# Moving the last four shifted pieces of the first token mix into the plan that orders the attention

## The chip, the cores and the metric

The kernel runs on one core of one Trainium2 chip. Its time is the device time of one execution in microseconds (us); the engines named below are those of that core: TensorE (PE; its weight loads are PEld), VectorE (DVE), ScalarE (ACT), GpSimd (POOL) and SyncE (SP), which issues the transfers (DMA) in queue order.

## What is computed

Three stages in a row. First an attention over 2 batches x 8 heads, 768 tokens, head size 64, with a mask made of hashed sign bits; then a channel mix with a shift by one token; then a low-rank mix over the tokens and a wide two-layer network.

```python
mask = q_bucket[:, :, :, None] == k_bucket[:, :, None, :]
scores = np.where(mask, scale * q @ k.T, -1e9)          # softmax, then @ v -> x [2, 768, 512]
x_prev = x shifted down by one token
xk = mu_k * x + (1.0 - mu_k) * x_prev
xr = mu_r * x + (1.0 - mu_r) * x_prev
k = np.maximum(xk @ w_k, 0.0)                           # 512 -> 1024
v = k * k @ w_v                                         # 1024 -> 512
x = sigmoid(xr @ w_r) * v
u = x + (x.T @ U @ V).T
out = u + np.maximum(u @ w_ch1, 0.0) @ w_ch2            # 512 -> 2048 -> 512
```

The inputs q, k, v and the weights come as 64-bit words or 32-bit floats. A product of 32-bit accuracy is made of three products of halves: high x high, high x low, low x high.

## The kernel before, in words

**Attention.** 16 heads x 6 tiles of 128 query rows. For each head q and k are loaded (`nq`, `nk`), split into halves (`hl_q`, `hl_k`), transposed by TensorE and copied to `yq`, `yk`; `xq`, `xk` and `zt` hold the rows with the bits. These are the prepared q and k, which only the scores (L521, L522) read. The results of two heads form one block of 128 features of x, `xn`, which TensorE transposes (L616) in two steps of three products each; ScalarE evicts each step to `xT` (L389). All these transposes go through one PSUM bank, tag `t`, which is free again only after the eviction.

**The plan.** Everything up to the end of the attention is added to a list of operations (`Plan.add`) with engines and costs, dependences, buffers taken and freed, and a due time: the place in the attention plus an offset from the table `DUE` by kind. `Plan.order` walks through time and gives each free engine the ready operation with the smallest due time. The program is then written in that order, and every engine runs its own part strictly in it. Where the plan sees a gap of TensorE it adds idle products (L332) in number to the gap's length.

**The first mix, its shifted pieces.** For batch 0 there are 16 pieces `(s, g, c)`: `s` is r or k (xr or xk), `g` a half of the tokens (384), `c` one of four blocks of 128 features. A piece takes four instructions: a scaling of the shifted x (`shift_scaled`, L716 on ScalarE or L718 on VectorE) into an `xs_a` buffer of the tag `sq` (3 buffers, shared with the activations below), the sum on VectorE (`shift_sum`, L722), the high half on ScalarE (`shift_high`, L737) and the low half (`shift_low`, L180, on POOL or VectorE). The plan holds the first twelve: r of both halves, and k of the first half. The last four, k of the second half of the tokens, are called k1c0 to k1c3 here. The pool `xh2` holds their halves, and it is opened after the attention's pools are closed.

**The first mix, its products.** Units u = 0 to 15: `m = u // 2` is a block of 128 of the 1024 hidden features, `g = u % 2` the half of the tokens. A k half, k(u), is 12 products of 384 columns (3 for each `c`); ScalarE makes a relu and a square, POOL the exact square, VectorE the low half (L796); a v half, v(u), is nine products of 512 columns, of which the third is the first to read the low half. The order is k(0), k(2), v(0), k(1), v(2), k(3), v(1), and so on, so that k(1) is the first to read k1c0 to k1c3. They are made by a loop that stands between k(0) and the rest:

```python
mix.acc()
k_half(mix, 0, True)
while mix.todo or mix.begun:
    shifts(mix, nc.gpsimd if len(mix.todo) % 2 else None)
halves(mix, u1, range(1, U1 - 2), ...)
```

**Weights.** They arrive as 64-bit words in 512 KB loads (`raw`, 3 buffers) and are converted in jobs: ScalarE two scalings (L224, L225), VectorE two steps on the bits (L229, L233), POOL a sum (`cx`, L180), ScalarE the high half (L273), VectorE or POOL the low half. The jobs run as a chain: with each k half of the mix one step of four jobs and one load is taken ("tick"). The plan converts jobs 0 to 7, which serve w_r and the units 0 to 3, and starts the next ones; the first tick, in k(0), has the halves of job 8, the sum of job 9, the bits of job 10, the scalings of job 11 and the load of job 12, which goes into the buffer that the sum of job 9 frees.

Of the kernel before, what the change touches and what calls it, by code (L numbers as in the profile page):

```python
# [22 lines left out]
PE_TILES = (1, 4)  # L23
# [6 lines left out]
JOB_GATE = (0, 0, 1, 1, 2, 3, 4, 5)  # L30
JOBS = 8
VG = 4
FILL, FIRST_FILL = 0.85, 34
SLOTS = {"s": 3, "t": 1, "o": 1, "n": 4, "hl_q": 1, "hl_k": 1, "y_q": 2, "y_k": 2, "x_q": 2, "x_k": 2, "zt": 2,
         "p": 3, "p12": 4, "pT": 6, "xn": 2, "raw": 3, "cx": 4, "xh": 4, "sq": 3, "v": 2, "nm": 4, "nv": 6}
# [94 lines left out]
def lsh_attention_moe_kernel(  # L130
# [19 lines left out]
    nc = tc.nc  # L150
# [150 lines left out]
    def load_head(i, s, eng=None):  # L301
        b, h = heads[i]
        src = {"k": k, "q": q, "v": v}[s]
        if s == "v":
            t = NV[i % len(NV)][:, :, 0:D]
        else:
            t = hd[i]["n" + s] = ap.tile([128, NT, D], F32, tag=f"n{s}", name=f"n{s}")
        (eng or nc.sync).dma_start(out=t, in_=src[b, h].rearrange("(p t) d -> p t d", t=NT))
# [67 lines left out]
    big = ap.tile([VG, 128], F32, name="big", bufs=1)  # L376
# [21 lines left out]
    def prep_H(i, s, e):  # L398
        t = hd[i]["hl" + s] = ap.tile([128, NT, 2, D], F32R, name=f"hl_{s}", bufs=1)
        copy(e, t[:, :, PART[s]], hd[i]["n" + s])  # L400
# [19 lines left out]
    def prep_E(i, s, g, e):  # L420
        if g == 0:
            hd[i]["y" + s] = ap.tile([128, S], F32R, tag=f"y{s}", name=f"y{s}")
        copy(e, hd[i]["y" + s][:, g * G:(g + 1) * G], hd[i].pop(("t" + s, g)))

    def first_E(s, e):
        hd[0]["y" + s] = ap.tile([128, S], F32R, tag=f"y{s}", name=f"y{s}")
        copy(e, hd[0]["y" + s].rearrange("p (g c) -> p g c", g=NG), hd[0]["both" + s][:, :, 0:G])

    def first_x(s, e):
        t = hd[0]["x" + s] = ap.tile([MC, S], F32R, tag=f"x{s}", name=f"x{s}")  # L430
        copy(e, t[LOW].rearrange("p (g c) -> p g c", g=NG), hd[0].pop("both" + s)[HI[s], :, 0:G])
# [10 lines left out]
    def prep_x(i, s):  # L442
        t = hd[i]["x" + s] = ap.tile([MC, S], F32R, tag=f"x{s}", name=f"x{s}")
        nc.sync.dma_start(out=f(t)[LOW], in_=f(hd[i]["y" + s])[HI[s]])
# [10 lines left out]
    def prep_bits(i):  # L455
        zt = hd[i]["zt"] = ap.tile([ZE, G], F32R, tag="zt", name="zt")
# [10 lines left out]

    vg = [{} for _ in range(NH // VG)]

    def v_max(i):  # L470
        g, j = divmod(i, VG)
        if j == 0:
            vg[g]["max"] = ap.tile([128, VG], F32, tag="vmax", name="vmax")
        nc.vector.tensor_reduce(
            out=vg[g]["max"][:, j:j + 1], in_=NV[i % len(NV)][:, :, 0:D], axis=AX.XY, op=ALU.max, apply_absolute_value=True
        )

    def v_flip(g):
# [12 lines left out]
    def v_spread(g):
        vg[g]["u"] = psum_t()
        nc.tensor.matmul(vg[g]["u"][:, 0:VG], big, vg[g].pop("pow"), start=True, stop=True)

    def v_scale(g):
        sc = vg[g]["scale"] = ap.tile([128, VG], F32, tag="vsc", name="vsc", bufs=3)
        nc.vector.tensor_copy(sc, vg[g].pop("u")[:, 0:VG])

    def v_scale_of(i):
        g, j = divmod(i, VG)  # L500
        return vg[g]["scale"][:, j:j + 1]
# [11 lines left out]

    def scores(n):
# [52 lines left out]

    def flip_out(n, e):
        pT = tl[n]["pF"] = ap.tile([128, NT, 128], F32, tag="pT", name="pF", bufs=SLOTS["pT"])
        copy(e, pT.rearrange("p (j i) c -> p j (i c)", j=NG), tl[n].pop("f")[:, :, 0:G])  # L570


    def weighted(n):
# [4 lines left out]
        if t in PE_TILES:  # L578
# [340 lines left out]
    for i in range(NH):  # L919
# [38 lines left out]
        g, j = divmod(i, VG)  # L958
# [3 lines left out]
        if j == VG - 1:  # L962
            at0 = g * VG * NT - 4
            t_s, u_s = Slot("t"), Slot("t")
            fl = add({"pe": 0.2}, lambda e, g=g: v_flip(g), v_mx[-VG:], at0, take=[t_s], lag=0.25)
# [3 lines left out]
            for ii in range(g * VG, i + 1):  # L969
                v_s2, nv_s2 = v_slots[ii]  # L970
                v0 = v0_of[ii] = add({"act": 0.62}, lambda e, i=ii: prep_v(i, 0), [v_sc, v_ld[ii]], ii * NT - 0.5, "v1")
                v1 = add({"act": 0.53}, lambda e, i=ii: prep_v(i, 1), [v0], ii * NT, "v1", [v_s2])
                v2_of[ii] = add({"pool": 0.98}, lambda e, i=ii: prep_v(i, 2), [v1], ii * NT, "v2", free=[nv_s2])
    for i in range(NH):
# [3 lines left out]
        for t in range(NT):  # L978
# [9 lines left out]
            if t in PE_TILES:  # L988
# [3 lines left out]
                got = add({"act": 0.83, "dve": 0.86}, lambda e, n=n: flip_out(n, e), [fl], n, "f1", [pT_s], [f_s])  # L992
# [5 lines left out]
            on_pe = t in PE_TILES  # L998
            avs.append(add({"pe": 0.9 if on_pe else 0.62}, lambda e, n=n: weighted(n), [got, v0_of[i] if on_pe else v2], n, "av",
# [37 lines left out]
    for j, (s, g, c) in enumerate(todo := mx0.todo[0:3 * KD]):  # L1037
        a_s = Slot("sq")
        if c == 0:
            x_s = [Slot("xh") for _ in range(KD)]  # L1040
# [3 lines left out]
        hi = add({"act": 0.53}, lambda e, p=p: hold.append(mx0.shift_high(*p)), [sm, hi and low_of[todo[j - 1]]], at, kind, [x_s[c]])  # L1044
# [19 lines left out]
    mx0.todo = mx0.todo[3 * KD:]  # L1064
# [8 lines left out]
    late["xh2"] = pool(mix_s, "xh2", side="right", bufs=4)  # L1073
# [38 lines left out]
    while mix.todo or mix.begun:  # L1112
        shifts(mix, nc.gpsimd if len(mix.todo) % 2 else None)
# [111 lines left out]
```

## Time and profile before

| what | value |
|---|---|
| three runs of the kernel | 728.95, 730.35, 734.12 us; median 730.35 |
| the profiled execution | 728.76 us, of which the span from first to last instruction is 727.0 |
| busy share of the span | PE 97%, PEld 84%, DVE 61%, ACT 53%, POOL 48% |
| mean granted clock of TensorE | 0.995 of 2.4 GHz |
| chain that ended last | PE 75%, DVE 8%, POOL 5%, DMA 4%, issue 4%, ACT 3% |

Times in rows are us from the span's start. In a timeline row stand start, length, engine, line, operation, what is written from what, shape and count, and in brackets the idle time just before it with what ended it. A waits row names who waited for whom, then the total, the number of waits and the longest. A windows row has the stretch, its length, the busy time (and count) of PE, PEld, DVE, ACT and POOL, then the granted clock (1.00 is 2.4 GHz, 0.50 is 1.2 GHz), the DMA share and GB/s. Starts are those of the profiler; the length of a TensorE product is modelled, so its pace is read from start to start.

### The profile page before, as it was taken

What the parts mean: (1) busy time and instruction counts of PE and PEld (TensorE: products, weight loads), DVE (VectorE), ACT (ScalarE), POOL (GpSimd) and SP (SyncE); (2) the same over time, 40 slices, a digit from 0 to 9 for tenths busy, and PEclk for the clock granted to TensorE, in tenths of its full rate; (3) what the DMA queues carried; (4) which work ended last, traced back from release to release, by engine and by line L of the source; (5) the groups of instructions that cost most, each with busy time, mean ns of one, the idle gap of its engine ahead of it and who ended that gap; (6) DMA issues with size and microseconds to landing.
All of it is one profiled execution on the core that took longest, in us unless ns stands there. A gap on an engine that the chain in (4) does not pass through costs nothing.

```text
span 727.0 us, 12722 instructions
## 1 busy us (share of the span) xinstructions
PE 707.1 (97%) x4907; PEld 612.1 (84%) x4907; DVE 440.6 (61%) x791; ACT 385.2 (53%) x651; POOL 351.1 (48%) x309
## 2 busy tenths in 40 slices
PE   9899999999999998999999999999999999999997
PEld 8798999999999886889788888778888888888886
DVE  7987888677776656898879978655532111321112
ACT  5887888688878666666478566434421001110100
POOL 5998888787969855566357544613300000000000
PEclk9999999999999999899999999999999999999999
DMA  7899899996987961322013332323201000010001
GB/s 189 194 177 198 190 198 205 167 175 148 174 182 144 208 114 58 116 75 92 2 59 115 116 114 63 125 77 109 65 0 59 1 0 1 1 58 1 0 1 58
DMA packets 140715, 73.23 MB, mean 101 GB/s; under 512 B 116832, under 2 KB 134064, under 8 KB 140656
## 3 DMA queue, kind: packets, MB, share of 16 engines
q1 hardware_dynamic: 140512, 72.24, 43.2%
q8 instruction: 38, 0.62, 0.3%
q10 hardware_dynamic: 144, 0.20, 0.1%
q14 instruction: 21, 0.17, 0.1%
HBM read 37.10 MB, written 3.15 MB: 55 GB/s over the span
## 4 chain that ended last, share of the span: by engine, by line
PE 75%; DVE 8%; POOL 5%; DMA 4%; issue 4%; ACT 3%; SPq 0%; POOLq 0%; ACTq 0%; DVEq 0%
PE ps L807 9%; PE pt L807 9%; PE ps L809 9%; PE pt L809 9%; PE pt L808 9%; PE ps L808 9%; PE pt L581 3%; DMA pT<-p 3%; PE pt L587 3%; PE ps L521 3%; POOL p L180 2%; PE ps L522 2%; PE pt L453 2%; DVE w L180 2%; PE pt L415 1%
## 5 line engine op out<-in xcount | busy, mean ns | idle before, releaser
L882 DVE SCALAR_TENSOR_TENSOR hl<-pt,hl 128x512 fp32r<-128x512 f32 x48 | 33.2, 691 | 170.9 <-ACT hl L881 170.9
L881 ACT ACTIVATE hl<-pt 128x512 fp32r<-128x512 f32 x48 | 28.7, 598 | 185.1 <-PE pt L809 185.1
L809 PE MATMUL ps<-w,hl 128*128 128x512 f32 x288 | 114.3, 397 | 3.3 <-DVE hl L796 3.1
L807 PE MATMUL ps<-w,hl 128*128 128x512 f32 x288 | 115.7, 402 | 0.1
L808 PE MATMUL ps<-w,hl 128*128 128x512 f32 x288 | 113.9, 395 | 0.0
L180 POOL TENSOR_TENSOR cx<-cx,raw 128x512 int32<-128x512 int32 (+2 forms) x55 | 80.4, 1461 | 65.2 <-DVE cx L233 59.2
L180 POOL TENSOR_TENSOR p<-p,p 128x768 f16<-128x768 f32 x64 | 108.0, 1693 | 7.8 <-ACT p L389 5.9
L526 DVE TENSOR_REDUCE nm<-ps 128x1 f32<-128x768 f32 x96 | 90.5, 952 | 17.3 <-PE ps L522 15.9
L540 ACT ACTIVATE p<-ps,nm 128x768 f32<-128x768 f32 x96 | 92.9, 988 | 11.7 <-DVE nm L534 10.3
L807 PE MATMUL pt<-ut,w 128*128 128x512 f32 x192 | 75.6, 394 | 0.0
L809 PE MATMUL pt<-ut,w 128*128 128x512 f32 x192 | 75.0, 391 | 0.0
L808 PE MATMUL pt<-ut,w 128*128 128x512 f32 x192 | 75.0, 391 | 0.0
L521 PE MATMUL ps<-xk,xq 76*128 76x384 f32 x192 | 70.6, 368 | 1.9 <-ACT p L540 1.2
L809 PEld LDWEIGHTS ps<-w,hl 128*128 128x128 f32 x288 | 54.5, 189 | 19.2 <-DVE hl L796 7.1
L807 PEld LDWEIGHTS ps<-w,hl 128*128 128x128 f32 x288 | 54.5, 189 | 14.1 <-issue 1.7
L180 DVE TENSOR_TENSOR w<-cx,w 128x512 fp32r<-128x512 f32 (+2 forms) x52 | 61.2, 1177 | 8.2 <-ACT w L273 7.7
L522 PE MATMUL ps<-yk,yq 128*128 128x384 f32 x192 | 65.1, 339 | 0.0
L808 PEld LDWEIGHTS ps<-w,hl 128*128 128x128 f32 x288 | 54.6, 190 | 10.3
L229 DVE SCALAR_TENSOR_TENSOR raw<-raw 128x512 uint32<-128x512 uint32 (+2 forms) x55 | 54.2, 985 | 0.0
L180 POOL TENSOR_TENSOR sq<-sq 128x384 f32<-128x384 f32 x32 | 32.0, 1000 | 38.2 <-ACT hl L791 37.2
L391 POOL CAST p<-p 128x768 f16<-128x768 f32 x49 | 41.3, 843 | 17.1 <-ACT p L540 15.8
L587 PE MATMUL pt<-v,pT 128*128 128x65 f16 (+1 forms) x1152 | 45.7, 194 | 2.5 <-DMA pT<-p 2.5
(181 smaller groups left out, 1511.5 us busy)
## 6 DMA issues: line engine op xcount, KB each, us to landing
raw<-in_moe_w_ch_dram SPq DMA_DIRECT2D x32, 512.0 KB
raw<-in_moe_w_k_dram SPq DMA_DIRECT2D x8, 512.0 KB
raw<-in_moe_w_v_dram SPq DMA_DIRECT2D x8, 512.0 KB
nk<-in_k_dram SPq DMA_DIRECT2D x16, 192.0 KB
nv<-in_v_dram SPq DMA_DIRECT2D x16, 192.0 KB
nq<-in_q_dram SPq DMA_DIRECT2D x15, 192.0 KB
xk<-yk SPq DMA_DIRECT2D x15, 192.0 KB
xq<-yq SPq DMA_DIRECT2D x15, 192.0 KB
```

Of the source, the lines that this page charges most:

```text
L180: eng.tensor_tensor(out=out, in0=a, in1=b, op=op)
L229: nc.vector.scalar_tensor_tensor(out=raw[:, :, 0], in0=raw[:, :, 1], scalar=0x80000000, in1=raw[:, :, 0], op0=ALU.bitwise_and, op1=ALU.bit ...
L391: (nc.vector if e == "dve" else nc.gpsimd).tensor_copy(dst, src)
L521: nc.tensor.matmul(s_ps[:, j, 0:G], d["xq"][:, qc], d["xk"][:, c], start=True, stop=False)
L522: nc.tensor.matmul(s_ps[:, j, 0:G], d["yq"][:, qc], d["yk"][:, c], start=False, stop=True)
L526: nc.vector.tensor_reduce(out=nm[:, 0:1], in_=tl[n]["s"][:, :, 0:G], axis=AX.XY, op=ALU.max, negate=True)
L540: nc.scalar.activation(p, tl[n].pop("s")[:, :, 0:G], AF.Exp, bias=nm[:, 2:3], scale=nm[:, 1:2])
L587: nc.tensor.matmul(o[:, 0:d], pT[:, part, kt, :], V[:, kt, a, 0:d], start=(kt == 0 and (part, a) == (0, 0)), stop=(kt == NT - 1 and part = ...
L807: nc.tensor.matmul(o, sh, mh, start=first, stop=False)
L808: nc.tensor.matmul(o, sh, ml, start=False, stop=False)
L809: nc.tensor.matmul(o, sl, mh, start=False, stop=last)
L882: nc.vector.scalar_tensor_tensor(out=hl[:, 1], in0=self.o, scalar=0.0, in1=f(hl)[:, 0], op0=ALU.max, op1=ALU.subtract)
```

## The change

All sixteen pieces of batch 0 are now in the plan. The last four have the kind `m3`, whose offset 900 puts them behind everything else that is ready. Their halves still go to the pool `xh2`, which is now opened, on the other side of the memory, in the moment in which the last scores are written into the program: the prepared q and k have a pool of their own (`prep`) that is closed there, and the high halves of the last four pieces carry a dependence on all scores and flips (`last_s`). The loop behind k(0) is gone.

```diff
-       "r4": -59.5, "r5": -145.5}
+       "r4": -59.5, "fw": 4.7, "f2": 0, "m3": 900, "r5": -145.5}
...
+    prep_s = ExitStack()
     ap = pool(att, "att", side="right", bufs=2)
+    pp = pool(prep_s, "prep", side="right", bufs=2)
...
     def scores(n):
...
+        scored.append(n)
+        if len(scored) == NH * NT:
+            prep_s.close()
+            late["xh2"] = pool(mix_s, "xh2", bufs=4)
...
-    for j, (s, g, c) in enumerate(todo := mx0.todo[0:3 * KD]):
+    for j, (s, g, c) in enumerate(todo := mx0.todo):
         a_s = Slot("sq")
         if c == 0:
-            x_s = [Slot("xh") for _ in range(KD)]
+            far = (s, g) == ("k", 1)
+            x_s = [Slot("xh2" if far else "xh") for _ in range(KD)]
         at, kind, p = 2 * c, f"m{j // KD}", (s, g, c)
         begun = [add({"act": 0.6 if g else 0.85}, lambda e, p=p: mx0.shift_scaled(*p, e == "act"), begun, at, kind, [a_s])]
         sm = add({"dve": 1.1}, lambda e, p=p: mx0.shift_sum(*p), begun, at, kind)
-        hi = add({"act": 0.53}, lambda e, p=p: hold.append(mx0.shift_high(*p)), [sm, hi and low_of[todo[j - 1]]], at, kind, [x_s[c]])
+        hi = add({"act": 0.53}, lambda e, p=p: hold.append(mx0.shift_high(*p)), [sm, hi and low_of[todo[j - 1]], *(last_s if far else [])],
+                 at, kind, [x_s[c]])
         low_of[p] = add({"pool": 1.05}, lambda e, p=p: mx0.shift_low(*p, hold.pop(), nc.gpsimd), [hi], at, kind, free=[a_s])
...
-    mx0.todo = mx0.todo[3 * KD:]
+    mx0.todo = []
...
-    late["xh2"] = pool(mix_s, "xh2", side="right", bufs=4)
...
     mix.acc()
     k_half(mix, 0, True)
-    while mix.todo or mix.begun:
-        shifts(mix, nc.gpsimd if len(mix.todo) % 2 else None)
     halves(mix, u1, range(1, U1 - 2), ...)
```

The rest of the diff renames: `PE_TILES = (1, 4)` becomes `MODES` with the same two tiles on TensorE, `VG = 4` becomes `GROUPS = (4, 4, 4, 4)`, the tiles `n`, `hl`, `y`, `x` and `zt` of q and k are taken from `prep`, and the scale of v has four buffers instead of three. A third way for a tile ("F") is written and not used.

On ScalarE, at the attention's end, the rows before run from the high half of the third k piece (`xh`) over four evictions (`xT`) to the high half of weight job 8 (`w`) and the relu of k(0) (`sq`):

```order
L737 ACTIVATE xh_4827<-xs_a_4646 128x384
L389 ACTIVATE xT_154<-pt_4831 128x384
L737 ACTIVATE xh_4854<-xs_a_4797 128x384
L389 ACTIVATE xT_154<-pt_4857 128x384
L389 ACTIVATE xT_154<-pt_4879 128x384
L389 ACTIVATE xT_154<-pt_4894 128x384
L273 ACTIVATE w_4937<-cx_4588 128x512
L790 ACTIVATE sq_4942<-pt_4924 128x384
```

The same place on ScalarE after the change, from the high half of the fourth k piece to the high half of job 8 (the scaling of k1c0 stands just ahead of the first of the four evictions, which is the one before these rows):

```order
L764 ACTIVATE xh_4864<-xs_a_4804 128x384
L743 ACTIVATE xs_a_4871<-xT_154,omu_k_326 128x384
L391 ACTIVATE xT_157<-pt_4867 128x384
L764 ACTIVATE xh_4879<-xs_a_4837 128x384
L743 ACTIVATE xs_a_4905<-xT_154,omu_k_326 128x384
L391 ACTIVATE xT_157<-pt_4901 128x384
L764 ACTIVATE xh_4931<-xs_a_4871 128x384
L743 ACTIVATE xs_a_4933<-xT_155,omu_k_326 128x384
L391 ACTIVATE xT_157<-pt_4927 128x384
L764 ACTIVATE xh_4938<-xs_a_4905 128x384
L764 ACTIVATE xh_4941<-xs_a_4933 128x384
L275 ACTIVATE w_4979<-cx_4591 128x512
```

A scaling and a high half now stand ahead of each of the last three evictions, and two high halves ahead of the weights.

On POOL the rows before run from the low half of the fourth k piece over the sum of job 9 (`cx`) and the square for k(0) (`sq`) to two of the last four pieces, the sum of job 10 and the square for k(2):

```order
L180 TENSOR_TENSOR xh_4854<-xs_a_4797,xh_4854 128x384
L180 TENSOR_TENSOR cx_4657<-cx_4657,raw_4477 128x512
L180 TENSOR_TENSOR sq_4942<-sq_4942 128x384
L180 TENSOR_TENSOR xh_4960<-xs_a_4954,xh_4960 128x384
L180 TENSOR_TENSOR xh_4972<-xs_a_4963,xh_4972 128x384
L180 TENSOR_TENSOR cx_4674<-cx_4674,raw_4479 128x512
L180 TENSOR_TENSOR sq_4996<-sq_4996 128x384
```

The same place on POOL after the change:

```order
L180 TENSOR_TENSOR xh_4864<-xs_a_4804,xh_4864 128x384
L180 TENSOR_TENSOR xh_4879<-xs_a_4837,xh_4879 128x384
L180 TENSOR_TENSOR xh_4931<-xs_a_4871,xh_4931 128x384
L180 TENSOR_TENSOR xh_4938<-xs_a_4905,xh_4938 128x384
L180 TENSOR_TENSOR xh_4941<-xs_a_4933,xh_4941 128x384
L180 TENSOR_TENSOR cx_4664<-cx_4664,raw_4480 128x512
L180 TENSOR_TENSOR sq_4984<-sq_4984 128x384
L180 TENSOR_TENSOR cx_4681<-cx_4681,raw_4482 128x512
L180 TENSOR_TENSOR sq_5014<-sq_5014 128x384
```

All four low halves, two of which were VectorE's, stand ahead of the sum of job 9 and the square for k(0). On VectorE the four sums stand ahead of the weights of job 8 now, one of them ahead of the last head's normalisation; two scalings and two low halves are gone from it. TensorE has 7 idle products more ahead of each of the last two pairs of transposes (28 rows with their weight loads), and nothing else moved on it. SP's order is the same.

## Rows read from the trace of the kernel before

**Rows 1.** The page: busy time, share of the span and instructions of each engine.

```profile
PE 707.1 (97%) x4907; PEld 612.1 (84%) x4907; DVE 440.6 (61%) x791; ACT 385.2 (53%) x651; POOL 351.1 (48%) x309
```

**Rows 2.** Waits of TensorE over the whole span: total, times, longest.

```profile
PE ps L809 <- DVE hl L796: 3.1, 5, 0.9
```

**Rows 3.** Timeline of PE, 274 to 301 us, end of attention and first mix.

```profile
274.81 0.69 PE L332 MATMUL pt<-steady 128*128 128x120 f16 x10
...
275.56 0.55 PE L616 MATMUL pt<-ident,xn 128*128 128x128 f32 x3
...
275.86 0.42 PE L807 MATMUL pt<-xh,w 128*128 128x384 f32 x1
...
280.13 0.39 PE L807 MATMUL ps<-w,hl 128*128 128x512 f32 x1
...
280.97 0.50 PE L809 MATMUL ps<-w,hl 128*128 128x512 f32 x1 [0.22 <-DVE hl L796]
...
282.68 0.34 PE L807 MATMUL pt<-xh,w 128*128 128x384 f32 x1
...
288.42 0.63 PE L807 MATMUL ps<-w,hl 128*128 128x512 f32 x1
...
293.42 0.52 PE L807 MATMUL pt<-xh,w 128*128 128x384 f32 x1
...
296.01 0.40 PE L807 MATMUL ps<-w,hl 128*128 128x512 f32 x1
...
300.15 0.39 PE L807 MATMUL ps<-w,hl 128*128 128x512 f32 x1
```

**Rows 4.** Windows of 1 us: the granted clock in the first mix.

```profile
287.00:288.00 1.00, 0.42 (x2) 0.38 (x2) 1.00 (x2) 0.97 (x4) 0.15 (x1) 0.83 0.00 0
...
288.00:289.00 1.00, 1.00 (x4) 0.75 (x3) 1.00 (x3) 1.00 (x2) 0.87 (x1) 0.50 0.79 147
...
294.00:295.00 1.00, 1.00 (x6) 1.00 (x6) 1.00 (x1) 0.00 (x0) 1.00 (x1) 0.75 0.27 93
```

**Rows 5.** Timeline of ACT: last eviction, a scaling, a high half.

```profile
276.14 0.49 ACT L389 ACTIVATE xT<-pt 128x384 f32<-128x384 f32 x1 [0.64 <-PE pt L616]
...
280.37 0.60 ACT L716 ACTIVATE xs_a<-xT,omu_k 128x384 f32<-128x384 f32 x1
...
282.64 0.52 ACT L737 ACTIVATE xh<-xs_a 128x384 fp32r<-128x384 f32 x1
```

**Rows 6.** Timeline of POOL, 273 to 290 us: lows, weight sums, squares.

```profile
273.13 1.00 POOL L180 TENSOR_TENSOR xh<-xs_a,xh 128x384 fp32r<-128x384 f32 x1 [2.98 <-ACT xh L737]
...
274.08 1.29 POOL L180 TENSOR_TENSOR cx<-cx,raw 128x512 int32<-128x512 int32 x1
...
279.50 0.83 POOL L180 TENSOR_TENSOR sq<-sq 128x384 f32<-128x384 f32 x1 [4.13 <-ACT hl L791]
...
282.26 1.22 POOL L180 TENSOR_TENSOR xh<-xs_a,xh 128x384 fp32r<-128x384 f32 x1 [1.93 <-ACT xh L737]
...
285.53 1.62 POOL L180 TENSOR_TENSOR cx<-cx,raw 128x512 int32<-128x512 int32 x1
...
288.13 1.33 POOL L180 TENSOR_TENSOR sq<-sq 128x384 f32<-128x384 f32 x1 [0.98 <-POOL cx L180]
```

**Rows 7.** Timeline of DVE, 280 to 294 us: low halves, piece sums, weight low.

```profile
280.36 0.56 DVE L796 TENSOR_TENSOR hl<-sq,hl 128x384 fp32r<-128x384 f32 x1 [1.54 <-POOL sq L180]
...
281.99 1.91 DVE L722 SCALAR_TENSOR_TENSOR xs_a<-xT,mu_k,xs_a 128x384 f32<-128x384 f32 x2
...
290.13 1.78 DVE L180 TENSOR_TENSOR w<-cx,w 128x512 fp32r<-128x512 f32 x1
...
293.40 0.55 DVE L796 TENSOR_TENSOR hl<-sq,hl 128x384 fp32r<-128x384 f32 x1
```

**Rows 8.** Timeline of SP: the load of weight job 12.

```profile
275.40 0.38 SPq L212 DMA_DIRECT2D raw<-in_moe_w_k_dram  x1
```

**Rows 9.** Windows: a stretch of the attention with a long TensorE hole.

```profile
60.00:62.00 2.00, 0.56 (x16) 0.40 (x14) 0.00 (x0) 0.81 (x1) 1.73 (x3) 1.00 1.05 112
```

More of the change, by code (lines that the diff above doesn't have):

```diff
@@ L21 @@
 P_SHIFT = 12.0 * math.log(2.0)
-PE_TILES = (1, 4)
+MODES = ("DWDDWD", "DWDDWD")
 DUE = {"ld": -28.3, "h": 7, "lo": 111.2, "tr": -11.5, "es": -25.5, "xs": 92.5, "z": -68.8, "bits": 0,
@@ L375, in lsh_attention_moe_kernel @@
         V2.append(t)
-    big = ap.tile([VG, 128], F32, name="big", bufs=1)
+    big = ap.tile([max(GROUPS), 128], F32, name="big", bufs=1)
     nc.gpsimd.memset(big, 2.0 ** 13)
@@ L455, in prep_bits @@
     def prep_bits(i):
-        zt = hd[i]["zt"] = ap.tile([ZE, G], F32R, tag="zt", name="zt")
+        zt = hd[i]["zt"] = pp.tile([ZE, G], F32R, tag="zt", name="zt")
         nc.vector.tensor_scalar(
@@ L466, in prep_mask @@
             )
-    vg = [{} for _ in range(NH // VG)]
+    vg = [{} for _ in GROUPS]
+    vg_of = [(g, j) for g, n in enumerate(GROUPS) for j in range(n)]
+    VG = max(GROUPS)
     def v_max(i):
-        g, j = divmod(i, VG)
+        g, j = vg_of[i]
         if j == 0:
@@ L566, in flip, with mode @@
                 nc.tensor.transpose(f_ps[:, j, c], p[:, j, c], ident)
+    def mode(n):
+        return MODES[n // (NT * H)][n % NT]
     def flip_out(n, e):
@@ L570, in flip_out, with flipped, flip_part1, flip_part2 @@
         copy(e, pT.rearrange("p (j i) c -> p j (i c)", j=NG), tl[n].pop("f")[:, :, 0:G])
+    def flipped(n, part):
+        return tl[n]["pT"][:, part].rearrange("p (j i) c -> p j (i c)", j=NG), tl[n]["f"][:, :, 0:G]
+    def flip_part1(n):
+        pT_tile(n)
+        p1, src = flipped(n, 0)
+        nc.scalar.activation(p1, src, AF.Copy)
+    def flip_part2(n):
+        p1, src = flipped(n, 0)
+        minus("dve", flipped(n, 1)[0], src, p1)
+        tl[n].pop("f")
     def weighted(n):
@@ L968, in lsh_attention_moe_kernel @@
             v_sc = add({"dve": 0.15}, lambda e, g=g: v_scale(g), [sp], at0, free=[u_s])
-            for ii in range(g * VG, i + 1):
+            for ii in range(i0, i + 1):
                 v_s2, nv_s2 = v_slots[ii]
@@ L987, in lsh_attention_moe_kernel @@
             ex = add({"act": 1.02}, lambda e, n=n: exps(n), [bi], n, "ex", [p_s], [s_s, nm_s])
-            if t in PE_TILES:
+            kind = mode(n)
+            if kind in "FW":
                 f_s = Slot("s")
@@ L991, in lsh_attention_moe_kernel @@
                 last_s.append(fl)
-                got = add({"act": 0.83, "dve": 0.86}, lambda e, n=n: flip_out(n, e), [fl], n, "f1", [pT_s], [f_s])
+            if kind == "F":
+                p1 = add({"act": 0.83}, lambda e, n=n: flip_part1(n), [fl], n, "f1", [pT_s])
+                got = add({"dve": 0.97}, lambda e, n=n: flip_part2(n), [p1], n, "f2", free=[f_s])
+            elif kind == "W":
+                got = p1 = add({"act": 0.83, "dve": 0.86}, lambda e, n=n: flip_out(n, e), [fl], n, "fw", [pT_s], [f_s])
             else:
@@ L997, in lsh_attention_moe_kernel @@
                 got = add({"sp": 2.2}, lambda e, n=n: transp(n), [p2], n, "T", [pT_s], [c_s], issue=1.45)
-            on_pe = t in PE_TILES
-            avs.append(add({"pe": 0.9 if on_pe else 0.62}, lambda e, n=n: weighted(n), [got, v0_of[i] if on_pe else v2], n, "av",
+            avs.append(add({"pe": 0.9 if kind == "W" else 0.62}, lambda e, n=n: weighted(n), [got, v0_of[i] if kind == "W" else v2], n, "av",
                            [] if avs else [o_s], [pT_s, v_s, v_slots[i][1]], lag=0.25))
```

47 lines of the change are left out of this document (25 added, 22 removed).

## The prediction

> **What bounds the kernel now.** I read the page's busy line first: TensorE is busy for 97% of the span [rows 1], so only a stretch in which it stands still, or runs at half clock, has time to give. The list of TensorE's waits came next; its largest entry is the second product of a mix, which waits for VectorE's low half of the activations [rows 2]. The PE timeline shows where such holes lie close together: at the head of the first mix. The reader should see six half units there (name: what it multiplies): k(0) and k(2) from 275.86 to 280.13, v(0) to 282.68, k(1) to 288.42, v(2) to 293.42, k(3) to 296.01 [rows 3]. After it the rhythm is steady: 296.01 to 300.15 is one v and one k, 4.14 us, 2.07 each [rows 3]. Six halves at this pace are 12.4 us; they took 20.15. So 7.7 us are lost: 3.67 in k(1) (5.74 instead of 2.07), 2.93 in v(2), 0.52 in k(3), and the rest in v(0) and ahead of it.
>
> k(1) is the first half that reads the four moved pieces, and they are made between k(0) and k(1), on engines that convert weights and split activations at the same time. v(2) and k(3) suffer from what follows: the granted clock is 0.83 in 287:288, 0.50 from 288 on and 0.75 in 294:295 [rows 4], that is 1.2 instead of 2.4 GHz after the stretch in which TensorE kept stopping in k(1). v(2) itself waits at most 0.9, the longest of the waits of that line [rows 2]; without that and the 2.07 it has 2.0 left, which with k(3)'s 0.52 makes some 2.5 us for the clock.
>
> **The change part by part.** The tables that were rewritten (MODES, GROUPS) hold the old values, and the order of all five engines is the old one up to the end of the attention: no cost and no gain there. The scale's fourth buffer and the two pools cost nothing that a row could show.
>
> *Removed.* Behind k(0) stood four pieces: four scalings, sums, high halves and low halves, two scalings and two lows of them on VectorE. With them gone k(1), v(2) and k(3) find operands that are ready, if nothing else is late. Worth at most the 7.7 us.
>
> *Added to the attention's end, on ScalarE.* Between the four last evictions to xT now stand the scalings (0.60 each) and high halves (0.52) [rows 5]. Up to the second eviction they fit beside TensorE's last weighted products. Two groups of idle products grow by 7 each, ahead of the third and the fourth transposes; ten take 0.69 in the row [rows 3], so 14 are at most 0.97. The fourth transposes waited for the third eviction before, so part of their 7 lies beside that wait. The evictions themselves can be some tenths late behind a 0.52 or a 0.60. I take 0.6 us; the ends are 0.35 (one group's products alone) and 1.2. k(0) then begins at 276.46 instead of 275.86, and v(0) could begin at 276.46 + 4.27 = 280.73, with its third product, the first that reads a low half, at 281.2.
>
> *Moved on POOL: the new wait.* All four low halves stand ahead of the sum of weight job 9 and of the square for k(0), where two stood behind them. The fourth eviction began at 276.14, 0.58 after its transposes [rows 3, 5]; now 276.7, done at 277.2. Then ScalarE's last two high halves, to about 277.7 and 278.2. POOL's third low begins at 277.7 and its fourth at 278.7. From there:
> - lows: 1.00 each where VectorE rested, 1.22 beside it [rows 6]: the fourth ends at 279.7, at most 280.2;
> - the sum of job 9: 1.29, or 1.62 in the crowded stretch [rows 6]: 281.0 to 281.8;
> - the square: 0.83, or 1.33 [rows 6]: 281.8 to 283.1;
> - VectorE's low half: TensorE's third product of v(0) came 0.61 after that instruction's start (280.36, 280.97) [rows 3, 7]: 282.4 to 283.7.
>
> Before, the square ended at 280.33 and the third product ran at 280.97. So v(0) now stops where it hardly stopped: a hole of 1.2 to 2.5 us. I take 282.8, nearer the lower end, because the crowding of 285 to 289 came from VectorE's own pieces, which are gone. VectorE has weight work between, and one such subtraction can take 1.78 [rows 7]; the upper end covers it.
>
> *Behind the wait.* On POOL the next weight sums stand behind the square; on VectorE the next weight pair and the low half of k(2) stand behind the low half of k(0). For v(2) at 282.8 + 1.71 + 2.07 = 286.6 VectorE has 3.8 us, and the row of one crowded turn (290.13 to 293.40, the next low half) is 3.3 [rows 7]: no wait. The moved steps issue no DMA of their own. But SP's load of the next weight waits for the sum of job 9, since its buffer comes free there: it went out at 275.40 [rows 8], some 5.6 us later now. Its reader stands behind k(2)'s activations on ScalarE, near 282.7, and may wait; what it feeds is used several halves later, so the price is 0, and up to 1 if that wait holds k(1)'s activation back.
>
> *The sum.* Third product at 282.8, 1.71 to the end of v(0) as before (280.97 to 282.68), then three halves of 2.07: k(3) ends at 290.7 instead of 296.01. The gain is **5.3 us**, with ends 4.4 (283.7) and 5.9 (282.4 and 0.3 less at the head). What follows is bound by TensorE at the pace of rows 3, so nothing gives the gain back. The profiled execution took 728.76 (span 727.0): 728.76 - 5.3 = 723.5. It lies 1.6 us below the median of the three runs, 730.35; from the median the forecast is **725.1 us**.
>
> One row needs weighing. Two of VectorE's sums took 1.91 while POOL made a low half, whose own time was 1.22 instead of 1.00 [rows 6, 7]. The Trainium skill (SBUF — State Buffer, on the shared port pair) says that a VectorE instruction with two SBUF inputs and a GpSimd one exclude each other: the later blocks until the first is through. By the row two meetings cost POOL 0.2 each; by the rule each meeting may cost it a whole sum of VectorE, and the hole would lie at the upper end, 283.7, or 4.4 us of gain.
>
> **Rivals.**
> 1. *The clock falls all the same.* The hole at v(0) comes after the idle products and is one piece of about 1.6 us. If it brings 1.2 GHz, v(2) and k(3) pay 2.5 as before: gain 2.8, **727.6 us**. For it: the fall of rows 4 came after holes of this kind of total. Against: in the attention TensorE was busy for only 0.56 of the 2.00 us from 60 to 62, and the granted clock stayed at 1.00 [rows 9]; k(1) had such holes one after another for 5.7 us. The Trainium skill (TensorE: Matmul & The Clock Gate, on the HAM clock gate) has half clock as the resting state that activity lifts; by it the fall is possible, and the row of 60 to 62 shows a hole of this size that did not bring it.
> 2. *No hole.* If POOL and VectorE are quicker than their rows, or the square slips through in time, only the 0.6 at the head is lost: gain 7.1, **723.2 us**.
> 3. *Slower: the attention's end becomes a series.* ScalarE runs in order and one PSUM bank carries all four transposes. If a high half waits there for a sum that has only just begun (0.60 + 0.95 + 0.52 = 2.07) and the next scaling for the buffer that a low half frees (1.22), two such turns ahead of the fourth eviction hold k(0) by 6.6 us. TensorE has only idle products there, the clock falls (2.5), and the later losses of 7.7 go: 6.6 + 2.5 - 7.7 = +1.4, **731.8 us**. It decides from a delay of 5.2 us on. For it: every high half does wait for VectorE. Against: the pieces read batch 0, complete long before, and VectorE stands idle between the last normalisation and the weights.
> 4. *It changes nothing.* The pieces are early, but the conversion chain, 5.6 us late at job 9, holds the halves of the first units instead, and k(3) ends where it did: gain 0 to 1, about **729.9 us**. Against: the jobs that the plan did cover the first four units.
>
> **How the numbers follow.** Chances: forecast 0.63, clock falls 0.13, no hole 0.12, slower 0.06, nothing 0.06. The likeliest case's own range, 4.4 to 5.9 us of gain, is 724.4 to 726.0; the shown runs spread from 728.95 to 734.12, so I widen it. The range **721.5 to 729.0** takes in the rivals 1 and 2 and leaves out 3 and 4. One per cent, about what a measurement of this kernel can tell from no change, is 7.3 us: faster than 723.05 needs nearly the whole loss. I give that 0.14 (half of rival 2, and 0.08 of the forecast for the spread of runs); slower by over 1% (above 737.65) 0.03, the far end of rival 3; within 1% 0.83.
>
> **What would show it.** Right: on the PE timeline k(1) runs 2.1 us without a stop, a hole of 1 to 2.5 us stands in v(0) ahead of its third product with VectorE's low half as releaser, POOL shows four lows in a row and then the sum and the square, and the clock stays at 1.00 from 287 to 295 on the old scale. Wrong in size: the hole is gone, or over 3 us, or the clock row shows 0.50 again. Wrong in kind: k(0) begins over 2 us late, with evictions waiting behind high halves, or a k half later than k(3) waits for a weight.

## The result and the profile after

| what | before | after |
|---|---|---|
| median of the timed runs (range) | 729.65 us, 6 runs (728.24 to 734.12) | 738.06 us, 6 runs (735.01 to 740.62) |
| ratio after / before | | 1.0103, 95% interval 1.0066 to 1.014 |
| profiled execution (its span) | 728.76 us (727.0) | 738.12 us (736.0) |

The change made the kernel slower, by some 7.5 us; 725.1 was predicted, with a range of 721.5 to 729.0. The profiled executions of three experiments below (e1_scale3, f1_before_scale11, g1_scale3_again) were disturbed ones; of these only the clock and the first mix of e1_scale3 are read, and ratios leave disturbed runs out.

The page of after, busy shares, the main DMA queue and the chain that ended last (compare [rows 1]; before, the queue was at 43.2% and DMA was 4% of the chain):

```profile
PE 709.8 (96%) x4921; PEld 617.2 (84%) x4921; DVE 439.7 (60%) x787; ACT 385.8 (52%) x653; POOL 353.4 (48%) x311
...
q1 hardware_dynamic: 140512, 72.24, 43.7%
...
PE 74%; DMA 8%; POOL 6%; DVE 5%; issue 3%; ACT 3%; SPq 0%; POOLq 0%; DVEq 0%; ACTq 0%
```

TensorE's busy time is 2.7 us longer and the span 9 us. Where, its timeline at the end of the attention and in the first mix tells. First the second step of transposes before, which [rows 3] do not reach:

```profile
272.69 0.55 PE L616 MATMUL pt<-ident,xn 128*128 128x128 f32 x3
273.85 0.79 PE L332 MATMUL pt<-steady 128*128 128x120 f16 x12 [0.61 <-DVE xn L606]
```

Then after, with starts some 14 us later:

```profile
286.47 0.55 PE L643 MATMUL pt<-ident,xn 128*128 128x128 f32 x3
287.63 1.16 PE L334 MATMUL pt<-steady 128*128 128x120 f16 x19 [0.62 <-DVE xn L633]
288.63 0.50 PE L643 MATMUL pt<-ident,xn 128*128 128x128 f32 x3
288.96 1.06 PE L334 MATMUL pt<-steady 128*128 128x120 f16 x17
289.86 0.50 PE L643 MATMUL pt<-ident,xn 128*128 128x128 f32 x3
290.11 0.42 PE L834 MATMUL pt<-xh,w 128*128 128x384 f32 x1
...
294.38 0.39 PE L834 MATMUL ps<-w,hl 128*128 128x512 f32 x1
294.61 0.40 PE L835 MATMUL ps<-w,hl 128*128 128x512 f32 x1
297.20 0.50 PE L836 MATMUL ps<-w,hl 128*128 128x512 f32 x1 [2.19 <-DVE hl L823]
...
298.92 0.34 PE L834 MATMUL pt<-xh,w 128*128 128x384 f32 x1
...
301.03 0.39 PE L834 MATMUL ps<-w,hl 128*128 128x512 f32 x1
...
305.20 0.39 PE L834 MATMUL ps<-w,hl 128*128 128x512 f32 x1
```

The two groups of idle products are there with 7 more each, the hole stands ahead of v(0)'s third product, and k(1) runs from 298.92 to 301.03 without a stop. k(3) ends at 305.20: the six halves take 15.09 us where they took 20.15. The second step of transposes began at 272.69 before and begins at 286.47 now; from there to k(0) it is 3.64 us instead of 3.17, and to the end of k(3) 18.73 instead of 23.32. So the part that the change moves is 4.6 us shorter, and all that is lost is lost before that step: it comes 13.8 us later. The windows up to it, before and after (stretch, length, busy time of PE, PEld, DVE, ACT, POOL, granted clock, DMA share, GB/s):

```profile
0.00:272.69 272.69, 263.01 (x2884) 246.73 (x2884) 208.31 (x475) 209.95 (x335) 223.22 (x208) 1.00 0.88 178
```

```profile
0.00:286.47 286.47, 269.80 (x2884) 253.34 (x2885) 205.58 (x476) 210.47 (x336) 222.04 (x208) 0.99 0.87 169
```

The same 2884 products keep TensorE busy for 269.80 us instead of 263.01, and it is idle for 16.7 us instead of 9.7: about half of the 13.8 us is waiting, and the other half goes into products that take longer. The DMA engines bring fewer bytes per second at the same share.

Engine order there is the old one. What differs is whom TensorE waits for. Its waits for a DMA before, total, times and longest:

```profile
PE pt L587 <- DMA pT<-p: 2.5, 4, 1.4
```

and its two largest waits in after:

```profile
PE pt L614 <- DMA pT<-p: 8.3, 7, 2.4
PE ps L836 <- DVE hl L823: 4.5, 5, 2.2
```

The second line is the hole in v(0) and smaller waits like those of [rows 2]. The first has most of the new waiting, 5.8 of the 7.0 us: a weighted product (p x v) waits for `pT`, the probabilities that a DMA transpose brings from `p12`. The view of the tile `pT`, first before, then after, adds the waits of TensorE's products and those of its weight loads, which overlap:

```profile
L555 SPq DMA_TRANSPOSE pT<-p x64: 1304/1801/4887, 21.2 to 264.4; - x64
...
  DMA pT<-p: 6.0, 9
```

```profile
L566 SPq DMA_TRANSPOSE pT<-p x64: 1304/1870/4117, 24.4 to 278.2; - x64
...
  DMA pT<-p: 18.3, 15
```

6.0 us in 9 waits (2.5 and 3.5) have become 18.3 in 15 (8.3 and 10.0). The first transpose is 3.2 us late already; that belongs to this execution and not to the change (f3_pT_off below, which takes the time of before, starts its first at 24.3 as well).

### The profile page after: what moved, and what is told of

Same layout as the page of the kernel before. It is cut to its first block, busy times and chain, and to the rows that moved or that the text cites. A ratio compares the mean times of both kernels' runs of the same rounds, so it can differ in the third digit from the quotient of the medians.

```text
span 736.0 us, 12754 instructions
## 1 busy us (share of the span) xinstructions
PE 709.8 (96%) x4921; PEld 617.2 (84%) x4921; DVE 439.7 (60%) x787; ACT 385.8 (52%) x653; POOL 353.4 (48%) x311
## 4 chain that ended last, share of the span: by engine, by line
PE 74%; DMA 8%; POOL 6%; DVE 5%; issue 3%; ACT 3%; SPq 0%; POOLq 0%; DVEq 0%; ACTq 0%
PE ps L834 9%; PE ps L836 9%; PE pt L834 9%; PE ps L835 9%; PE pt L836 9%; PE pt L835 9%; DMA pT<-p 5%; PE pt L608 3%; PE pt L614 3%; POOL p L180 3%; PE ps L528 3%; PE ps L529 2%; PE pt L455 2%; PE ps L577 2%; POOL p L393 1%
## 5 line engine op out<-in xcount | busy, mean ns | idle before, releaser
L180 DVE TENSOR_TENSOR w<-cx,w 128x512 fp32r<-128x512 f32 (+2 forms) x52 | 62.9, 1209 | 5.4 <-ACT w L275 3.9
L835 PEld LDWEIGHTS ps<-w,hl 128*128 128x128 f32 x288 | 54.1, 188 | 10.2
L231 DVE SCALAR_TENSOR_TENSOR raw<-raw 128x512 uint32<-128x512 uint32 (+2 forms) x55 | 56.0, 1017 | 0.0
L614 PEld LDWEIGHTS <-pT 128*128 128x128 f16 x1152 | 40.5, 99 | 14.8 <-DMA pT<-p 10.0
```

Source lines behind the costliest of these rows:

```text
L180: eng.tensor_tensor(out=out, in0=a, in1=b, op=op)
L231: nc.vector.scalar_tensor_tensor(out=raw[:, :, 0], in0=raw[:, :, 1], scalar=0x80000000, in1=raw[:, :, 0], op0=ALU.bitwise_and, op1=ALU.bit ...
L614: nc.tensor.matmul(o[:, 0:d], pT[:, part, kt, :], V[:, kt, a, 0:d], start=(kt == 0 and (part, a) == (0, 0)), stop=(kt == NT - 1 and part = ...
L835: nc.tensor.matmul(o, sh, ml, start=False, stop=False)
```

## The experiments

What could the change do to a transfer in the attention? Among its lines is one of bookkeeping: the scale of v, `vsc`, which takes 32 bytes of each partition, gets a fourth buffer. `vsc` lies above `pT` and `p12` in the pool, and all that is below it now lies 32 bytes lower. In the compiled program of before the buffers of `p12` begin at byte 192256 of each partition, a multiple of 256, and those of `pT` at 204544, also one. In after they begin at 192224 and 204512. `p12` is the source of all 64 DMA transposes of the attention: 3072 bytes per partition, read in rows of 256.

**The theory:** the loss comes from where the transposes' source or target starts, and the first mix has gained as forecast. **Rivals:** an accident of the chip or run; a cost of the two pools and the plan's later end; the moved pieces disturb the attention itself.

### After once more, and with the old three buffers

The kernel after without any edit:

> The changed kernel once more, nothing edited. The attention's last transposes stood at 289.9 us in its first profile against 275.6 before; 3 of these 14 us arise in the first 13 us, where TensorE's products run at half clock, the rest between 50 and 160. Theory chance (the start's clock fell badly in that one execution and the rest follows from the other timing): the profile starts at full clock this time and the time is 733 to 735. Theory place (the attention's buffers lie 32 bytes off a multiple of 64) and theory pools (the other order of pools in memory, or the sums that come early): about 738 again, last transposes near 287 to 290.

734.24 us (10 runs) beside 730.80 (19 runs of before): ratio 1.0057, 1.0033 to 1.0081. In a second set of runs it is slower again, if by less. The median lies in the 733 to 735 that were named for chance, so this run alone does not decide. Its profiled execution took 738.73 us, with the last transposes at 290.47, near the 287 to 290 of the other theories, and has the same shape: six halves 15.08 us, hole 2.21.

```diff
-        sc = vg[g]["scale"] = ap.tile([128, VG], F32, tag="vsc", name="vsc", bufs=4)
+        sc = vg[g]["scale"] = ap.tile([128, VG], F32, tag="vsc", name="vsc", bufs=3)
```

> The changed kernel with three buffers instead of four for the scale of v, which moves every tile of the attention back by 32 bytes; the order of all engines is the same. Theory place: the attention is as long as before, the gain of the first mix is left, time 722 to 726, last transposes at 276 to 277. Theory pools: 737 to 739, as the pools still lie in the new order. Theory chance: 733 to 738, unrelated to the edit.

726.63 us (10 runs): ratio 0.9938, 0.9906 to 0.9971. That is 0.6 us above the range expected; the place of the last transposes is not read. With 32 bytes per partition less, and every moved piece where the change put it, the kernel is faster than before. That excludes the pieces and the plan as the cause of the loss.

### Before, with the buffers alone

`bufs=4` in before (32 bytes lower), then `bufs=5` (64 lower), with nothing else changed:

```diff
-        sc = vg[g]["scale"] = ap.tile([128, VG], F32, tag="vsc", name="vsc", bufs=3)
+        sc = vg[g]["scale"] = ap.tile([128, VG], F32, tag="vsc", name="vsc", bufs=4)
```

> The kernel before with four buffers for the scale of v: all tiles of the attention lie 32 bytes lower, nothing else changes. Theory place: the attention gets some 10 to 14 us longer, time 739 to 744. Theory pools and theory chance: 728 to 732, as before.

738.40 us (4 runs): ratio 1.0128, 1.0064 to 1.0192, a little under the 739 to 744 expected. A buffer that nothing needs costs before the whole loss.

> The kernel before with five buffers for the scale: the same tiles lie 64 bytes lower. Theory place: 728 to 732, since the starts are multiples of 64 again; if the loss were that of any shift, or of the number of scale buffers, it would be 739 to 744 like the version with four. Theory pools and theory chance: 728 to 732.

738.98 us (4 runs): ratio 1.011, 1.0072 to 1.0148. This expectation failed: a multiple of 64 bytes is as slow as one of 32. The place counts, but by a coarser step.

### Which step: 128 or 256 bytes

`bufs=11` puts `p12` and `pT` 256 bytes lower, `bufs=7` 128 lower.

> The kernel before with eleven scale buffers: all attention tiles 256 bytes lower, so that the sources and targets of the DMA transposes (p12 and pT) start at multiples of 256 as in the kernel before. Theory place, now read as a multiple of 256 or 128 for these two tiles: as before, 728 to 733, DMA queue 1 busy for 314 to 316 us (share times span), while the shifts by 32 and 64 had 323 to 325. Theory 'any more scale buffers, any shift costs': 736 to 741.

731.59 us (10 runs): ratio 1.0006, 0.9976 to 1.0036: no loss. The queue's time is not read here.

> The kernel before with seven scale buffers: the tiles 128 bytes lower. If starts at multiples of 128 are enough: 728 to 733 and 314 to 316 us of queue 1; if it takes multiples of 256: 735 to 741 and 321 to 325 us.

738.72 us (4 runs): ratio 1.0132, 1.0078 to 1.0186: the full loss, though with 318 us of queue 1, under the 321 to 325 expected. Of the five places tried (0, 32, 64, 128 and 256 below a multiple of 256) only the two multiples of 256 are free of it, so the amount of memory isn't the cause either: the largest shift costs nothing.

### Source or target

Two versions of before with empty tiles (cleared once, never read) between the buffers: one in which only `pT` is off by 32 bytes, one in which only `p12` is. The first takes `bufs=4` for `vsc` and puts 224 bytes between `p12` and `pT` (`p12` at 192000, `pT` at 204512). The second, shown here, puts 32 bytes between them and 224 below `p12` (192224 and 204544). In both, all that lies below is moved by 256 bytes in sum.

```diff
+    def pad(cols):
+        if cols and cols not in pads:
+            pads.append(cols)
+            nc.gpsimd.memset(ap.tile([128, cols], F32, name=f"pad{cols}", bufs=1), 0.0)
...
     def part1(n, e):
+        pad(56)
...
     def pT_tile(n):
+        pad(8)
```

> The kernel before with only the targets of the DMA transposes (pT) 32 bytes off a multiple of 256; their sources p12 and every tile below keep their place in 256, by an empty tile of 224 bytes that one small instruction clears. If the target's start counts: 736 to 741, queue 1 busy for 321 to 325 us. If the source's start counts, or that of another tile: 728 to 733 and 314 to 316 us.

729.60 us (10 runs): ratio 0.9999, 0.9973 to 1.0024; queue 1 was busy for 309 us, less than expected.

> The kernel before with only the sources p12 32 bytes off a multiple of 256; the targets pT and every tile below keep their place in 256, by two empty tiles. If the source's start counts: 736 to 741, queue 1 busy for 321 to 325 us. If the target's, or that of another tile: 728 to 733 and 314 to 316 us.

738.56 us (4 runs): ratio 1.0109, 1.0065 to 1.0153; queue 1 was busy for 324 us. The start of the source counts; that of the target does not. The pair differs by one clearing instruction, the number of scale buffers and places in memory, which makes it the place to see what the loss consists of. TensorE's waits for `pT` and three stretches of 40 us (columns as above), target off:

```profile
PE pt L597 <- DMA pT<-p: 2.1, 3, 1.6
```

```profile
60.00:100.00 40.00, 38.35 (x441) 37.10 (x440) 31.59 (x76) 31.79 (x52) 35.09 (x30) 1.00 0.95 198
100.00:140.00 40.00, 39.38 (x446) 37.81 (x445) 32.45 (x67) 33.30 (x52) 36.03 (x30) 1.00 0.96 202
140.00:180.00 40.00, 38.44 (x434) 36.50 (x433) 30.12 (x73) 31.57 (x55) 30.52 (x26) 1.00 0.85 165
```

and source off:

```profile
PE pt L597 <- DMA pT<-p: 8.3, 6, 2.6
```

```profile
60.00:100.00 40.00, 34.74 (x402) 33.35 (x402) 27.68 (x64) 28.91 (x46) 32.23 (x27) 0.96 0.97 178
100.00:140.00 40.00, 39.33 (x381) 37.89 (x381) 30.80 (x63) 30.68 (x48) 32.66 (x28) 0.91 0.91 181
140.00:180.00 40.00, 35.60 (x416) 33.67 (x414) 28.22 (x70) 29.08 (x49) 28.68 (x24) 1.00 0.92 165
```

The DMA engines are busy for 95% of the stretch from 60 to 100 even in the good version: there is hardly room for slower transposes. With the source off they bring fewer bytes for their busy time: 198 GB/s at 0.95 have become 178 at 0.97, 202 at 0.96 have become 181 at 0.91, and 165 at 0.85 have become 165 at 0.92. TensorE does 39 and 65 products fewer in the first two stretches, and its granted clock is at 0.96 and 0.91 where it was 1.00.

The clock is a part of what this execution lost. With the source off the second step of transposes begins at 284.69, 12.0 us later than before, in an execution whose first transpose goes out at 21.2 like that of before:

```profile
0.00:284.69 284.69, 268.09 (x2884) 251.38 (x2884) 206.77 (x475) 210.45 (x335) 223.18 (x210) 0.98 0.88 170
```

TensorE is idle for 16.6 us instead of 9.7 and busy for 268.1 instead of 263.0: 6.9 us of the 12.0 is waiting, and 5.1 goes into products that take longer. The granted clock was at 0.50 (1.2 GHz) for 10.2 us of this attention. Ahead of the first fall TensorE had stood almost still for two us:

```profile
62.00:64.00 2.00, 0.04 (x1) 0.04 (x2) 0.00 (x0) 0.00 (x0) 0.59 (x1) 0.87 1.15 68
64.00:66.00 2.00, 2.00 (x23) 2.00 (x24) 0.76 (x3) 0.00 (x0) 1.88 (x2) 0.50 1.07 334
```

The trace also has a record of every single DMA packet, and these show it by size. The rows of `p12` are 256 bytes long: 12 x 128 x 64 = 98,304 of the 110,592 packets of that size. Summed for that size and for all others (16 engines together), with the time that the granted clock was at 0.50 between 20 and 270 us, summed from windows of 1 us:

| kernel | `p12` above a multiple of 256 by | 256 B packets, us | of them over 18 ns | other packets, us | half clock, us | ratio to before |
|---|---|---|---|---|---|---|
| before | 0 | 2600 | 5.4% | 2487 | 0 | 1 |
| f3_pT_off | 0 | 2573 | 5.0% | 2442 | 0 | 0.9999 |
| g2_pools_only | 0 | 2556 | 5.7% | 2430 | 0 | 0.9995 |
| g3_after_p12_on | 0 | 2634 | 4.9% | 2462 | 0 | 0.9925 |
| g4_low_first | 0 | 2616 | 5.8% | 2437 | 0 | 0.9947 |
| f2_before_scale7 | 128 | 2713 | 14.6% | 2444 | 6.8 | 1.0132 |
| e3_before_scale5 | 192 | 2791 | 16.5% | 2435 | 10.2 | 1.011 |
| e2_before_scale4 | 224 | 2804 | 16.7% | 2449 | 6.8 | 1.0128 |
| f4_p12_off | 224 | 2799 | 15.3% | 2457 | 10.2 | 1.0109 |
| after | 224 | 2750 | 17.0% | 2461 | 6.8 | 1.0103 |
| e0_after_again | 224 | 2770 | 16.6% | 2493 | 10.2 | 1.0057 |

The packet of 256 bytes takes 18 ns in the median everywhere. Off the multiple three times as many take longer, and only this size changes: 2713 to 2804 us against 2556 to 2634. The means of the two groups, 2771 and 2596, lie 175 us apart, 11 us on each of 16 engines. The loss in time is 8.0 to 9.6 us (1.1 to 1.3% in the four versions of before), of the same size. All six executions with the source off have half clock in the attention, none of the five others in the table. It can come without the place, too: e1_scale3 has the source on, and in its profiled execution, of 735.26 us, the clock was at 0.50 for 17 us of the attention. That TensorE's longer waits for the transposes bring the falls is thus argued, and was not tried apart.

### The change without the loss

After with three buffers again, beside three others on one chip: the same with the last four pieces made behind k(0) as before, so that only the two pools and the plan's calls are left of the change; after with its four buffers and an empty tile of 224 bytes between `p12` and `pT`, so that the source starts at 192000 and the target is off; and a version in which the activations of k(0) and k(2) (with POOL's square and VectorE's low half) are issued ahead of the weight jobs.

> The changed kernel with three scale buffers once more, as its first profile fell on a slow execution (735.3 against a median of 726.6). Theory place (the start of p12 at a multiple of 256 decides the attention's length, the moved pieces give their gain in the first mix): median 725 to 727.5, from the first product of k(0) to the end of k(3) 15.1 us as in the changed kernel against 20.2 before, queue 1 busy for 309 to 318 us.

728.37 us (12 runs): ratio 0.996, 0.9939 to 0.9981; faster than before, but 0.9 us above the range expected. The halves and the queue are not read here.

```diff
+    while mix.todo or mix.begun:
+        shifts(mix, nc.gpsimd if len(mix.todo) % 2 else None)
     halves(mix, u1, range(1, U1 - 2), ...)
```

> The changed kernel with three scale buffers and with the last four pieces made behind k(0) again, so that every engine has the order of the kernel before: only the pools in memory are new. Theory place: 728 to 733, as the kernel before, and k(0) to k(3) take 19.6 to 21 us. Theory pools (the new pools cost or give something of their own): more than 3 us away from the kernel before.

730.57 us (10 runs): ratio 0.9995, 0.9974 to 1.0016; the six halves take 20.96 us. The pools and the plan's calls cost nothing that can be measured.

```diff
     def pT_tile(n):
+        pad(56)
         tl[n]["pT"] = ap.tile([128, 2, NT, 128], F16, tag="pT", name="pT", bufs=SLOTS["pT"])
```

> The changed kernel with its four scale buffers and an empty tile of 224 bytes that moves p12 to a multiple of 256 and leaves pT 32 bytes off. Theory place, source alone: 725 to 728, as with three scale buffers. If four scale buffers cost something of their own, or pT's start counts in this layout: 733 to 738.

725.68 us (4 runs): ratio 0.9925, 0.99 to 0.9949. So after, with its fourth buffer and all its moves, is the faster kernel once `p12` starts at a multiple of 256. Its six halves took 16.62 us in the profile, more than the 15.09 of after, and the 1-us windows (columns as above) say why:

```profile
282.00:283.00 1.00, 0.86 (x4) 0.73 (x5) 1.00 (x2) 0.00 (x0) 1.00 (x1) 1.00 0.88 306
283.00:284.00 1.00, 1.00 (x5) 0.83 (x4) 1.00 (x2) 0.27 (x1) 1.00 (x2) 0.78 0.03 10
284.00:285.00 1.00, 1.00 (x4) 0.90 (x4) 1.00 (x2) 1.00 (x3) 0.48 (x1) 0.50 0.82 266
285.00:286.00 1.00, 1.00 (x4) 1.00 (x4) 1.00 (x4) 0.50 (x2) 0.55 (x1) 0.50 0.71 254
```

After the hole in v(0) (2.17 us here) the granted clock is at 0.50, 1.2 GHz, for some 3 us. The first mix of e1_scale3 has the same: a hole of 2.20, the fall, six halves in 16.61. From the second step of transposes to the end of k(3) these two take 20.26 and 20.25 us where before took 23.32, a gain of 3.1 and not 4.6. In after the same hole of 2.19 brought no such fall, nor did that of e0_after_again:

```profile
296.00:297.00 1.00, 0.00 (x0) 0.00 (x0) 1.00 (x2) 0.73 (x2) 0.64 (x2) 1.00 0.61 143
297.00:298.00 1.00, 0.80 (x3) 0.67 (x4) 1.00 (x2) 0.00 (x0) 1.00 (x1) 1.00 1.03 364
298.00:299.00 1.00, 1.00 (x6) 0.82 (x5) 1.00 (x2) 0.29 (x1) 1.00 (x2) 1.00 0.05 17
```

```diff
+        early = mix is mixes[0] and u in (0, 2)
+        if early:
+            mix.k_act(u)
+            mix.k_low(u)
         if tick:
             tick_a()
-        mix.k_act(u)
+        if not early:
+            mix.k_act(u)
```

> The changed kernel with three scale buffers, and in the first two halves, k(0) and k(2), the activation and its low half are issued ahead of the weight work instead of around it. If the hole of 2.2 us in v(0) is POOL's queue (four lows, weight sum, square) and VectorE's (weight pair ahead of the low half), it closes: k(0) to k(3) 12.6 to 13.5 us instead of 15.1, time 722.5 to 725.5. If the third product waits for something else, or v(2) stops instead: 725 to 728.

726.16 us (12 runs): ratio 0.9947, 0.9925 to 0.9968, in the range expected if the hole does not close. The third product of v(0) in its profile:

```profile
280.90 0.40 PE L835 MATMUL ps<-w,hl 128*128 128x512 f32 x1
282.59 0.50 PE L836 MATMUL ps<-w,hl 128*128 128x512 f32 x1 [1.29 <-DVE hl L823]
```

The hole shrank from 2.19 to 1.29 us and the six halves to 14.19, not to the 12.6 to 13.5 expected. What is left of it shows on POOL and VectorE:

```profile
277.73 1.99 POOL L180 TENSOR_TENSOR xh<-xs_a,xh 128x384 fp32r<-128x384 f32 x2 [0.28 <-ACT xh L764]
280.04 0.83 POOL L180 TENSOR_TENSOR sq<-sq 128x384 f32<-128x384 f32 x1 [0.33 <-ACT hl L818]
280.83 1.29 POOL L180 TENSOR_TENSOR cx<-cx,raw 128x512 int32<-128x512 int32 x1
```

```profile
280.90 1.64 DVE L823 TENSOR_TENSOR hl<-sq,hl 128x384 fp32r<-128x384 f32 x1 [3.03 <-POOL sq L180]
```

POOL's lows are done at 279.72, before the operand of the square is there, so they are no longer in the way. The low half begins right behind the square but takes 1.64 us instead of the 0.55 in after: POOL's sum of job 9 began 0.07 us ahead of it, and the low half ends 0.42 us after that sum. These 1.09 us are most of the hole. The 0.9 us gained cannot be told apart in the time: the intervals of this version and of g1_scale3_again and g3_after_p12_on overlap, and TensorE's waits for low halves are 4.8 us in sum over the span, where after had 4.5. The weight work ahead of the square and of the low half was thus part of the hole; the edit moved POOL's and VectorE's share of it together, so they are not told apart.

## Why the prediction was wrong

**The step that failed** is this: "The tables that were rewritten (MODES, GROUPS) hold the old values, and the order of all five engines is the old one up to the end of the attention: no cost and no gain there. The scale's fourth buffer and the two pools cost nothing that a row could show." The order is the old one, the pools cost nothing (0.9995), and yet the fourth buffer, a term put at 0, costs 8.0 to 9.6 us, since it moves the source of the transposes. The prediction asked of a buffer what waits for it, not what lies below it. That DMA had little slack could be read before: its share of 0.88 over the attention and of 1.05 in [rows 9], and TensorE's 2.5 us of waits for `pT`. That the source's place matters could not be read from the trace of before.

**The rest, term by term.** On the scale of the prediction after's times of the first mix are 13.65 us less (k(0) at 290.11 for 276.46).

- *Head* (the delay of k(0) by the added steps): 0.6 forecast, 0.47 measured.
- *POOL's queue:* third low at 277.7 forecast, fourth done at 279.7, the sum at 281.0 to 281.8, the square at 281.8 to 283.1. POOL and VectorE in after:

```profile
291.44 2.00 POOL L180 TENSOR_TENSOR xh<-xs_a,xh 128x384 fp32r<-128x384 f32 x2 [0.28 <-ACT xh L764]
293.38 1.78 POOL L180 TENSOR_TENSOR cx<-cx,raw 128x512 int32<-128x512 int32 x1
295.11 1.28 POOL L180 TENSOR_TENSOR sq<-sq 128x384 f32<-128x384 f32 x1
```

```profile
292.69 1.30 DVE L180 TENSOR_TENSOR w<-cx,w 128x512 fp32r<-128x512 f32 x1 [1.11 <-ACT w L275]
293.91 1.80 DVE L231 SCALAR_TENSOR_TENSOR raw<-raw 128x512 uint32<-128x512 uint32 x1
295.64 1.04 DVE L235 TENSOR_SCALAR cx<-cx 128x512 uint32<-128x512 uint32 x1
296.60 0.55 DVE L823 TENSOR_TENSOR hl<-sq,hl 128x384 fp32r<-128x384 f32 x1
```

  That is 277.79, 279.79, 281.51 and 282.74: the lows came as forecast (1.00 each), the sum took 1.78, more than its crowded row (1.62), and the square 1.28, near its own (1.33) [rows 6].
- *Hole:* third product at 283.55, where 282.8 was taken and 282.4 to 283.7 allowed; between the square's end (296.39) and the low half (296.60) VectorE was still at the bits of a weight. The hole is 2.19 us, within 1.2 to 2.5. This term was mis-sized by 0.75 us: the crowding was put down to VectorE's own pieces, but its weight job crowds as well. Its three steps took 1.30, 1.80 and 1.04 here, and 0.68, 0.68 and 0.42 where POOL rested or came later (g4_low_first, from 282.46, 286.82 and 287.43). The meeting that the prediction weighed thus came out near its upper end of 283.7, but the engine that took longer beside the lows was VectorE; POOL's lows kept their 1.00.
- *After it:* 1.72 to the end of v(0), then 6.28 for three halves (1.71 and 6.21 forecast). The gain is 4.6 us for the 5.3 forecast, inside its bounds of 4.4 to 5.9, in this execution with full clock.
- *The load of job 12:* out at 295.19, right behind the sum as forecast. ScalarE waited for it, but no product did:

```profile
298.70 0.67 ACT L226 ACTIVATE cx<-raw 128x512 f32<-128x512 f32 x1 [1.95 <-DMA raw<-in_moe_w_k_dram]
```

**The rivals.** Rival 1 (the clock falls all the same) had 0.13; it did not come in after and e0_after_again and came in g3_after_p12_on and e1_scale3, two of four, at 16.62 - 15.09 = 1.5 us instead of 2.5. Rivals 2 and 4 fell: there is a hole, and k(3) ends earlier. Rival 3 put the slower side at the attention's end, as a series of evictions and pieces; k(0) came 0.47 us late there, not 6.6. The kernel is slower by a mechanism that was not among them. Placed well, the change gives 0.996, 0.9938, 0.9947 and 0.9925 (2.9 to 5.5 us; the third has the edit of g4_low_first as well), where 5.3 of 730.35 is 0.9927. That is mostly less than forecast, and the interval of g1_scale3_again leaves 0.9927 out; the falls of the clock that g3_after_p12_on and e1_scale3 show would do that, but no trace shows whether it was so in g1_scale3_again. With the loss of 8.0 to 9.6 the gains make +2.5 to +6.7, against +4.2 measured in e0_after_again and +7.5 at first, the latter a little outside.

## What to carry to other kernels

One more buffer in a pool moves every tile on one side of it: ask of such an edit which transfers read from there, and compare the start addresses of the sources of DMA transposes before and after. Where a change loses in a stretch whose instructions it does not touch, undo its bookkeeping alone first; here one digit held the loss, and the gain showed once it was set back. The faster kernel of this study is after with `p12` kept at a multiple of 256.

## What was not expected of the hardware

- The DMA transposes of this kernel, with rows of 256 bytes in SBUF, are slower when their source does not start at a multiple of 256 bytes: 64 transposes cost 1.1 to 1.3% of the kernel's time. 32, 64 and 128 bytes off cost about the same; the target's start, 32 bytes off, costs nothing (0.9999). Rows of other lengths were not tried. In the packet records the share over 18 ns rises from about 5% to 15 to 17%.
- The Trainium skill (DMA: Bandwidth & Descriptors, "How a descriptor splits into AXI transactions") says that a transaction has to start at a 256-byte boundary, so a descriptor that starts elsewhere also fetches unused bytes from the boundary below. The runs agree as far as sources go; that the extra fetch is the mechanism was not shown, and most packets off the boundary still take 18 ns.
- The granted clock was at 0.50 for 6.8 to 10.2 us of the attention in each of the six executions with the source off, and not at all in five of the six with it on that are read; the sixth is e1_scale3.
- A VectorE instruction of 0.55 us took 1.64 when a POOL sum of 1.29 had begun 0.07 us ahead of it (g4_low_first).
- The same hole of 2.2 us was followed by half clock in two executions and by full clock in two. The two with full clock have the source off; what decides it stays open, as does whether the sources of the other transfers (loads, copies of `zt` and `y`) gain by their place; that was not tried.
